# Agent attention and a PReLU layer on one core: sums of exponentials on GpSimd in place of products with ones

## The chip, the cores and the metric

The kernel runs on one core of a Trainium2 chip. The metric is the device time of one execution, in microseconds. Before the change it is 988.02 us, the median of three runs (987.69, 988.02 and 988.49).

## What is computed

Two batches of 12480 queries, keys and values with 128 channels, and 49 agents per batch. The agents gather the values by a softmax over the keys, and each query takes a softmax over the agents. The attention result goes through a layer with 2048 hidden units and a PReLU.

```python
a2k = sm(agents, k)             # softmax over 12480 keys, scale 1/sqrt(128)
agent_v = a2k @ v               # 49 x 128 per batch
q2a = sm(q, agents)             # softmax over 49 agents, per query
x = (q2a @ agent_v).reshape(24960, 128)
h = x @ w_in
g = np.maximum(h, 0.0) + alpha * np.minimum(h, 0.0)
out = g @ w_out
```

In the reference `sm` subtracts the maximum, takes the exponential, and divides by the sum plus 1e-9.

## The kernel before, in words

Because the attention result is linear in the exponentials, the kernel multiplies `agent_v` with `w_in` once per batch (tile `sab`, a rounded part and a remainder), and applies that to the exponentials of the queries. The division by the softmax sum is left to the end: the PReLU is positively homogeneous, so each output row is scaled by the reciprocal of its sum just before it is stored. All products use numbers split in a rounded part and a remainder (`qmh` and `qml` for the exponentials, `rh` and `rl` for the positive part of the hidden units, `wh` and `wl` for the weights).

**Groups, pairs and steps.** The 24960 queries are cut in 52 groups of 480 (`GT`). Two groups make a pair (26 pairs). A group is worked off in eight steps (`NM`), each with 256 of the hidden units, so that there are 416 steps, 16 in a pair. In step s the loop (L1214) emits, in this order: the tasks of `first` for s, `g1(s + 2)`, the tasks of `plan` for s, and `g2(s)`. `g1` (L958) multiplies exponentials with `sab` into a PSUM tile `h` with two buffers (L968), ScalarE takes the positive part `rh` (L974), and VectorE takes the remainder `rl` from `h` and `rh` (L975), which is the last reader of that buffer. `g2` (L980) multiplies `rh` and `rl` with the output weights and adds them up in `acc` over the eight steps (L990); after the last one it adds the linear part (L1001) and brings the sum of both halves to SBUF (L1006 on ScalarE, L1007 on VectorE, tile `os`).

**The chain of a pair.** What prepares the exponentials of pair k is a list of fifteen tasks, `q_chain`, with a list of steps relative to the first step of the pair, `CHAIN` (`CHAIN_0` and `CHAIN_1` for the first two pairs): transpose of the queries (L827), split (L838, L845: `ql`), logits on TensorE (L864), copy to SBUF (L872), a swap of the two halves of the partitions by DMA (L883) and its addition (L890), the maximum over the partitions on GpSimd (L894, `partition_all_reduce`), its subtraction (L899), two exponentials on ScalarE (L903, L908), the split (L912, tile `qml`), the sum (L923), its spread (L933 to L941), and the reciprocal (L946 to L951). `q_take`, `q_swap` and `q_spread` go to `first`, the others to `plan`. Both halves of the partitions hold the same logits after the swap and the addition.

**The sum.** `q_sum` multiplies the two parts of the exponentials with a matrix of ones on TensorE, in two halves of 64 partitions, so that each row of the result holds the sums; `q_spread` copies them from PSUM to the tile `qsum` on ScalarE, and one DMA on SP's queue brings them in a 128x32 tile, from which `q_rec` makes the reciprocals.

**The output.** For group g, `o_take` transposes `os` into `ot` (L1012), `o_scale` multiplies it with the reciprocals (L1017, both operands in SBUF), and `o_store` writes four pieces on SP's queue (L1035). `OUT` says how many steps after the group's end: 4 for `o_take`, 5 for `o_scale` of either group, and one more for `o_store`. Within the 16 steps of a pair, the scaling of its first group falls on step 13 and that of its second group on step 5 of the next pair.

**Beside it.** The first batch's keys and values are worked off ahead of the steps. Those of the second batch are spread over the steps from 16 on: keys in five blocks of 16 steps (transposes L538, products L552, L574, maxima L591), values in six (L618, L609, L632, products L650, L660). Every engine works off its queue in the order in which the tasks are emitted; the tile framework puts in the waits.

Of the kernel before, what the change touches and what calls it, by code (L numbers as in the profile page):

```python
# [9 lines left out]
F32 = mybir.dt.float32  # L10
F32R = mybir.dt.float32r
U32 = mybir.dt.uint32
AF = mybir.ActivationFunctionType
ALU = mybir.AluOpType
# [8 lines left out]
KEYS = (((1, 0), 6, 7), ((5, 3), 9, 14), ((9, 12), 14, 16))  # L23
VALUES = ((((0, 3, 1, 1), (3, 1, 4, 4)), 6), (((3, 0, 7, 8), (2, 8, 5, 6)), 10))
FOLD = (189, 195, 198, 202, 205, 206)
CHAIN = (-18, -16, -16, -14, -13, -13, -11, -10, -7, -6, -5, -5, 4, 5, 10)
CHAIN_0 = (-19, -18, -18, -11, -9, -6, 1, 6, 10, 15, 17, 19)
CHAIN_1 = (-14, -13, -13, -11, -10, -10, -10, -10, -8, -7, -5, -5, 4, 5, 10)
EARLY = (1, 3, 6, 6)
OUT = (4, 5, 5)  # L30


LAGS = (7, 12, 17, 20, 21, 24)
# [22 lines left out]
def kernel(  # L56
# [11 lines left out]
    nc = tc.nc  # L68
# [4 lines left out]
    P = 128  # L73
    HALF = 64
    NF = DFF // P
    GT = 480
    TB = GT // 32
# [13 lines left out]
    SCALE = 1.0 / math.sqrt(C)  # L91
# [5 lines left out]
    p1 = ctx.enter_context(tc.tile_pool(name="p1", bufs=1))  # L97
# [12 lines left out]
    def pair_tile(name, i=None):  # L110

        i = (step[0] // NM + 1) % 2 if i is None else i
        return late[i].tile([P, 2, 512], F32, tag="x", name=name)
# [21 lines left out]
    padb = const.tile([P, 1], F32, name="padb")  # L135
# [654 lines left out]
    NGT = B * NG  # L790
    gq = {}
# [20 lines left out]
    def flat(t):  # L812
        return t.rearrange("p h n -> p (h n)")
# [90 lines left out]
        gq["mh", k] = m  # L904

    def q_exp(k):
        e = gq["e", k] = gq.pop(("s", k))
        nc.scalar.activation(out=e, in_=e, func=AF.Exp, bias=padb, scale=SCALE)  # L908

    def q_split(k):  # L910
        m = p2.tile([P, 2, GT], F32R, tag="qml", name=f"qml{k}")
        nc.vector.tensor_tensor(out=m, in0=gq["e", k], in1=gq["mh", k], op=ALU.subtract)  # L912
        mh = gq.pop(("mh", k))
        gq.pop(("e", k))
        gq["mhl", k] = (m, mh)
        for i in range(2):
            gq["M", 2 * k + i] = (mh[:, i, :], m[:, i, :])

    def q_sum(k):
        t = gq["sum_ps", k] = pair_tile(f"qsum{k}")  # L920
        for n, x in enumerate(gq.pop(("mhl", k))):
            for i, (r0, r1) in enumerate(TILES):
                nc.tensor.matmul(  # L923
                    t[:, i, 0:GT], lhsT=ones[r0:r1, :], rhs=x[r0:r1, i, :],
                    start=n == 0, stop=n == 1,
                )

    def q_spread(k):
        if "sums" not in gq:
            t = gq["sums"] = p1m.tile([P, 1024], F32, tag="qsum", name="qsum")  # L930
            nc.gpsimd.memset(t[:, 2 * GT :], 1.0)
        t = gq["sums"]
        nc.scalar.copy(  # L933
            out=t[:, 0 : 2 * GT].rearrange("p (h n) -> p h n", h=2),
            in_=gq.pop(("sum_ps", k))[:, :, 0:GT],
        )

        x = p1m.tile([P, 32], F32, tag="qx", name=f"qx{k}")
        nc.sync.dma_start(
            out=x, in_=t.rearrange("(c o) (i j) -> c o i j", c=4, j=32)[:, 0, :, :]  # L940
        )  # L941
        gq["sum", k] = x

    def q_rec(k):
        t = p1m.tile([P, 32], F32, tag="qst", name=f"qst{k}")
        nc.vector.transpose(out=t, in_=gq.pop(("sum", k)))  # L946
        r = p2.tile([P, 2, TB, 1], F32, tag="qr", name=f"qr{k}")
        nc.vector.tensor_scalar(
            out=r.rearrange("p h t o -> p (h t o)"), in0=t[:, 0 : 2 * TB], scalar1=1e-9, scalar2=None, op0=ALU.add
        )  # L950
        nc.vector.reciprocal(out=r, in_=r)  # L951
        for i in range(2):
            gq["r", 2 * k + i] = r[:, i]
# [68 lines left out]
    def o_store(g):  # L1022
# [14 lines left out]
    q_chain = [  # L1037
        q_transpose, q_hi, q_lo, q_logits, q_take, q_swap, q_add, q_max,
        q_sub, q_exp_hi, q_exp, q_split, q_sum, q_spread, q_rec,
    ]  # L1040

# [5 lines left out]
    with tc.manual_schedule():  # L1047
# [10 lines left out]
        def at(s, f, *a):  # L1058
            plan.setdefault(s, []).append((f, a))
# [34 lines left out]
        for n in range(7):  # L1094
            load, ops = (load_win, narrow_win) if n < 4 else (load_wo, narrow_wo)
            s = SLABS[n]
# [11 lines left out]
        def more():  # L1108
            f = next(loads, None)
            if f is not None:  # L1110
                f[1](*f[2:])
            return f

        while n_in < N_IN:
            f = more()
            n_in += f[1] not in (q_load_rows, load_alpha, load_late)
        for s in range(max(plan) + 1):
            for f, a in plan.pop(s, ()):
                f(*a)
                if f.__name__ == "total" or f in (k_turn, k_mix):  # L1120
                    while True:
                        f = more()
# [5 lines left out]
        p1m = ctx.enter_context(tc.tile_pool(name="p1m", bufs=1))  # L1128
# [22 lines left out]
        for i2 in range(NGT // 2):  # L1151
            s0 = 2 * NM * i2
            if i2 == 0:
                at(10, q_sum, 0)
                pre(11, q_spread, 0)
                at(13, q_rec, 0)
                continue
            steps = CHAIN if i2 > 1 else CHAIN_1
            if i2 > 1:
                at(max(0, s0 - LEADS[2]), q_load, i2)  # L1160
            for f, i in zip(q_chain, steps):
                (pre if f in (q_take, q_swap, q_spread) else at)(s0 + i, f, i2)
        for g in range(NGT):
            s0 = g * NM
            at((g + 1) * NM + OUT[0], o_take, g)
            d = OUT[1 if g % 2 == 0 or g == NGT - 1 else 2]
            at((g + 1) * NM + d, o_scale, g)
            at((g + 1) * NM + d + 1, o_store, g)

# [86 lines left out]
```

## Time and profile before

| | |
|---|---|
| median of three runs | 988.02 us |
| lowest and highest run | 987.69 and 988.49 us |
| span of the profiled execution, first to last instruction | 985.9 us |
| TensorE, VectorE, ScalarE, GpSimd busy | 99%, 85%, 64%, 9% |
| mean granted TensorE clock | 0.998 |

The span is that of one profiled execution; the page lists no other time for it, and a run's time holds the launch and the end around such a span. Busy shares are averages over stages: a plain pair of groups, a pair with keys of the second batch beside it, and a pair with values beside it differ. Matmuls are pipelined and two of 64 rows run at once, so their listed durations overlap. Spans on GpSimd are rough.

### The profile page before, as it was taken

Reading aid. Unit: us, or ns where it says so; the run is one execution under the profiler, and the core shown is the slowest. Engines: PE = TensorE matmul, PEld = TensorE weight load, DVE = VectorE, ACT = ScalarE, POOL = GpSimd, SP = SyncE. Lnnn points to the kernel's source line nnn. Section 1 sums busy time; section 2 is a strip of 40 time slices with the busy share of each in tenths; the row PEclk is TensorE's granted clock in tenths of the full one; section 3 lists DMA queues with packets and bytes.
Section 4 is the critical chain, followed back from the end, with each engine's and each line's share of the span. In section 5 each row is a group of like instructions: output and inputs, shape, how many; then the busy total and the mean of one; then the engine's idle time right before and its main releaser. Section 6 shows DMA issues by size and latency. Waiting matters only on the chain.

```text
span 985.9 us, 21716 instructions
## 1 busy us (share of the span) xinstructions
PE 971.7 (99%) x9046; PEld 927.0 (94%) x9046; DVE 837.7 (85%) x1054; ACT 626.4 (64%) x779; POOL 89.8 (9%) x67
## 2 busy tenths in 40 slices
PE   8989999999999999999999999999999999999997
PEld 5658999999989999999987999999999999999997
DVE  7887988998899999999987788788878887888775
ACT  5765655655667767777765666666666666666563
POOL 0011011011011011001101101100110111011100
PEclk9999999999999999999999999999999999999999
DMA  9933354444234234234312222212221223121201
GB/s 342 361 51 63 65 84 87 81 70 88 42 75 80 62 73 95 45 70 95 65 31 44 42 51 41 53 37 46 52 53 31 42 55 56 35 41 33 42 11 31
DMA packets 281027, 69.51 MB, mean 71 GB/s; under 512 B 259119, under 2 KB 273953, under 8 KB 280929
## 3 DMA queue, kind: packets, MB, share of 16 engines
q1 hardware_dynamic: 279937, 68.00, 33.0%
q8 instruction: 71, 1.16, 0.5%
q10 hardware_dynamic: 992, 0.12, 0.1%
q14 instruction: 27, 0.22, 0.1%
HBM read 42.59 MB, written 12.78 MB: 56 GB/s over the span
## 4 chain that ended last, share of the span: by engine, by line
PE 94%; DVE 2%; DMA 2%; ACT 1%; issue 0%; SPq 0%; ACTq 0%
PE acc L990 55%; PE h L968 27%; PE lg L864 2%; PE kl L552 2%; PE acc L1001 2%; PE av L650 1%; PE qsum L923 1%; DMA kw<-in_k_dram 1%; DMA win<-in_moe_w_in_dram 1%; PE a_ps L726 0%; DVE red L414 0%; PE avw L471 0%; PE ktp L388 0%; PE lin_ps L784 0%; PE etp L451 0%
## 5 line engine op out<-in xcount | busy, mean ns | idle before, releaser
L975 DVE SCALAR_TENSOR_TENSOR rl<-h,rh 128x960 fp32r<-128x960 f32 x416 | 478.2, 1150 | 123.1 <-ACT rh L974 120.8
L974 ACT ACTIVATE rh<-h 128x960 fp32r<-128x960 f32 x416 | 404.3, 972 | 270.1 <-PE h L968 262.1
L968 PE MATMUL h<-qmh,sab 64*128 64x480 f32 x1664 | 401.3, 378 | 0.7 <-DVE rl L975 0.5
L990 PE MATMUL acc<-rh,wl 64*128 64x480 f32 x1664 | 400.3, 378 | 0.0
L990 PE MATMUL acc<-rh,wh 64*128 64x480 f32 x1664 | 398.0, 375 | 0.0
L990 PE MATMUL acc<-rl,wh 64*128 64x480 f32 x1664 | 313.2, 377 | 0.0
L968 PEld LDWEIGHTS h<-qmh,sab 64*128 64x128 f32 x1664 | 247.2, 185 | 7.5 <-DVE rl L975 2.5
L990 PEld LDWEIGHTS acc<-rh,wl 64*128 64x128 f32 x1664 | 246.9, 184 | 5.9 <-issue 2.3
L990 PEld LDWEIGHTS acc<-rh,wh 64*128 64x128 f32 x1664 | 247.6, 184 | 2.9
L990 PEld LDWEIGHTS acc<-rl,wh 64*128 64x128 f32 x1664 | 223.6, 184 | 3.2
L968 PE MATMUL h<-qml,sab 64*128 64x480 f32 x832 | 222.7, 377 | 0.0
L894 POOL PARTITION_ALL_REDUCE qm<-qs x26 | 85.6, 3293 | 768.0 <-DVE qs L890 731.3
L968 PEld LDWEIGHTS h<-qml,sab 64*128 64x128 f32 x832 | 128.0, 185 | 1.7 <-DVE qml L912 0.2
L1006 ACT COPY os<-acc 128x480 f32<-128x480 f32 x52 | 29.2, 561 | 33.8 <-PE acc L1001 33.6
L1007 DVE TENSOR_TENSOR os<-acc,os 128x480 f32<-128x480 f32 x52 | 33.9, 651 | 2.7 <-ACT os L1006 2.4
L1012 DVE STREAM_TRANSPOSE ot<-os 128x480 f32<-128x480 f32 x52 | 34.7, 668 | 0.0
L903 ACT ACTIVATE qmh<-qs,padb 128x960 fp32r<-128x960 f32 x26 | 28.5, 1097 | 9.2 <-DVE qs L899 9.2
L1017 DVE TENSOR_TENSOR ot<-ot,qr 128x480 f32<-128x480 f32 x52 | 33.6, 645 | 0.1
L899 DVE TENSOR_TENSOR qs<-qs,qm 128x960 f32<-128x960 f32 x26 | 29.8, 1148 | 0.5 <-POOL qm L894 0.5
L890 DVE TENSOR_TENSOR qs<-qs,qw 128x960 f32<-128x960 f32 x25 | 28.7, 1148 | 1.7 <-DMA qw<-qs 1.7
L912 DVE TENSOR_TENSOR qml<-qs,qmh 128x960 fp32r<-128x960 f32 x26 | 29.8, 1148 | 0.0
L827 DVE STREAM_TRANSPOSE qt<-qin 128x960 f32<-128x960 f32 x25 | 29.2, 1167 | 0.0
(172 smaller groups left out, 802.8 us busy)
## 6 DMA issues: line engine op xcount, KB each, us to landing
out_dram<-ot SPq DMA_DIRECT2D x206, 60.0 KB
qin<-in_q_dram SPq DMA_DIRECT2D x200, 60.0 KB
qw<-qs SPq DMA_DIRECT2D x50, 240.0 KB
kw<-in_k_dram SPq DMA_DIRECT2D x12, 512.0 KB
vw<-in_v_dram SPq DMA_DIRECT2D x12, 512.0 KB
kb<-in_k_dram SPq DMA_DIRECT2D x96, 64.0 KB
v<-in_v_dram SPq DMA_DIRECT2D x24, 256.0 KB
win<-in_moe_w_in_dram SPq DMA_DIRECT2D x4, 512.0 KB
```

The lines of the kernel that those rows point to most:

```text
L827: nc.vector.transpose(out=flat(t), in_=gq.pop(("in", k)).rearrange("p h t i -> p (h t i)"))
L894: nc.gpsimd.partition_all_reduce(flat(t), flat(gq["s", k]), P, ReduceOp.max)
L899: nc.vector.tensor_tensor(out=t, in0=t, in1=gq.pop(("m", k)), op=ALU.subtract)
L912: nc.vector.tensor_tensor(out=m, in0=gq["e", k], in1=gq["mh", k], op=ALU.subtract)
L968: nc.tensor.matmul(h[:, u, 0:GT], lhsT=w[a][r0:r1, f0 : f0 + P], rhs=x[r0:r1, :], start=n == 0, stop=n == 2,)
L974: nc.scalar.activation(out=rh, in_=h[:, :, 0:GT], func=AF.Relu)
L975: nc.vector.scalar_tensor_tensor(out=rl, in0=h[:, :, 0:GT], scalar=0.0, in1=rh, op0=ALU.max, op1=ALU.subtract)
L990: nc.tensor.matmul(acc[:, i, 0:GT], lhsT=a[r0:r1, 2 * m + u, :], rhs=x[r0:r1, u, :], start=m == 0 and n == 0, stop=False,)
L1006: nc.scalar.copy(out=t, in_=acc[:, 0, 0:GT])
L1007: nc.vector.tensor_tensor(out=t, in0=acc[:, 1, 0:GT], in1=t, op=ALU.add)
L1012: nc.vector.transpose(out=t.rearrange("p t i -> p (t i)"), in_=oo.pop(g))
L1017: nc.vector.tensor_tensor(out=t, in0=t, in1=gq.pop(("r", g)).to_broadcast([P, TB, 32]), op=ALU.mult)
```

## The change

`q_exp` writes the exponentials to a tile of their own for every pair but the first. `q_sum` of these pairs no longer multiplies with ones: a GpSimd copy of one column of `qml` makes GpSimd wait for the split, and a `partition_all_reduce` with addition over all 128 partitions follows and writes `qsum`. Since both halves hold the same numbers the result is twice the sum, and `q_rec` multiplies it by one half. `q_spread` keeps its DMA and loses its copy. `q_sum` moves from step 4 of the pair to step -5 (the step of the split, behind it), and `q_spread` from step 5 to step 1. The scaling of a pair's first group moves from five to nine steps after the group's end (from step 13 of the pair to step 1 of the next one), and its stores with it, except in the last pair.

```diff
-CHAIN = (-18, -16, -16, -14, -13, -13, -11, -10, -7, -6, -5, -5, 4, 5, 10)
+CHAIN = (-18, -16, -16, -14, -13, -13, -11, -10, -7, -6, -5, -5, -5, 1, 10)
-CHAIN_1 = (-14, -13, -13, -11, -10, -10, -10, -10, -8, -7, -5, -5, 4, 5, 10)
+CHAIN_1 = (-14, -13, -13, -11, -10, -10, -10, -10, -8, -7, -5, -5, -5, 1, 10)
-OUT = (4, 5, 5)
+OUT = (4, 9, 5)
...
     def q_exp(k):
-        e = gq["e", k] = gq.pop(("s", k))
-        nc.scalar.activation(out=e, in_=e, func=AF.Exp, bias=padb, scale=SCALE)
+        s = e = gq.pop(("s", k))
+        if k:
+            e = p1.tile([P, 2, GT], F32, tag="qm", name=f"qe{k}")
+        gq["e", k] = e
+        nc.scalar.activation(out=e, in_=s, func=AF.Exp, bias=padb, scale=SCALE)
...
+    def sums():
+        if "sums" not in gq:
+            t = gq["sums"] = p1m.tile([P, 1024], F32, tag="qsum", name="qsum")
+            nc.gpsimd.memset(t[:, 2 * GT :], 1.0)
+        return gq["sums"]
+
     def q_sum(k):
+        e = gq.pop(("e", k))
+        if k:
+            m, _ = gq.pop(("mhl", k))
+            gate = p1m.tile([P, 1], F32, tag="gate", name=f"gate{k}")
+            nc.gpsimd.tensor_copy(gate, m[:, 1, GT - 1 : GT])
+            nc.gpsimd.partition_all_reduce(sums()[:, 0 : 2 * GT], flat(e), P, ReduceOp.add)
+            return
         t = gq["sum_ps", k] = pair_tile(f"qsum{k}")
...
     def q_spread(k):
...
-        nc.scalar.copy(
-            out=t[:, 0 : 2 * GT].rearrange("p (h n) -> p h n", h=2),
-            in_=gq.pop(("sum_ps", k))[:, :, 0:GT],
-        )
+        t = sums()
+        if k == 0:
+            nc.scalar.copy(
+                out=t[:, 0 : 2 * GT].rearrange("p (h n) -> p h n", h=2),
+                in_=gq.pop(("sum_ps", k))[:, :, 0:GT],
+            )
...
         nc.vector.tensor_scalar(
-            out=r.rearrange("p h t o -> p (h t o)"), in0=t[:, 0 : 2 * TB], scalar1=1e-9, scalar2=None, op0=ALU.add
+            out=r.rearrange("p h t o -> p (h t o)"), in0=t[:, 0 : 2 * TB], scalar1=0.5 if k else 1.0, scalar2=1e-9,
+            op0=ALU.mult, op1=ALU.add,
         )
...
-            d = OUT[1 if g % 2 == 0 or g == NGT - 1 else 2]
+            d = OUT[1 if g % 2 == 0 and g < NGT - 2 else 2]
```

## Rows read from the trace of the kernel before

**Rows 1.** The page: busy us (share of the span) xinstructions of each engine.

```profile
PE 971.7 (99%) x9046; PEld 927.0 (94%) x9046; DVE 837.7 (85%) x1054; ACT 626.4 (64%) x779; POOL 89.8 (9%) x67
```

**Rows 2.** The chain that ended last, by line, share of the span.

```profile
by line: PE acc L990 55.4%; PE h L968 27.5%; PE lg L864 2.2%; PE kl L552 2.1%; PE acc L1001 1.9%; PE av L650 1.2%; PE qsum L923 1.2%; DMA kw<-in_k_dram 1.1%; DMA win<-in_moe_w_in_dram 0.7%; PE a_ps L726 0.5%; DVE red L414 0.5%; PE avw L471 
```

**Rows 3.** Busy time of each engine in three stretches: plain, keys, values.

```profile
core 0: us, PE busy (x) PEld busy (x) DVE busy (x) ACT busy (x) POOL busy (x), PEclk, DMA share, GB/s
596.70:630.00 33.30, 33.30 (x310) 33.27 (x308) 27.47 (x31) 21.13 (x23) 3.31 (x1) 1.00 0.26 47
161.10:199.80 38.70, 38.70 (x408) 38.62 (x407) 34.69 (x43) 22.63 (x26) 3.33 (x2) 1.00 0.48 81
311.60:346.70 35.10, 35.10 (x341) 35.04 (x338) 33.25 (x45) 25.69 (x35) 3.50 (x5) 1.00 0.36 74
```

**Rows 4.** Instructions of tile qsum: min/median/max ns, first and last start us, form.

```profile
L923 PE MATMUL qsum<-qml,ones x52: 372/378/383, 95.0 to 956.3; 64*128 64x480 f32 x52
L923 PE MATMUL qsum<-qmh,ones x52: 371/377/383, 95.2 to 956.5; 64*128 64x480 f32 x52
L933 ACT COPY qsum<-qsum x26: 942/954/958, 97.4 to 957.4; 128x960 f32<-128x960 f32 x26
```

**Rows 5.** Timeline of PE, plain pair: start us, us, engine, line, operation.

```profile
820.96 0.38 PE L968 MATMUL h<-qmh,sab 64*128 64x480 f32 x1
...
822.92 0.38 PE L968 MATMUL h<-qmh,sab 64*128 64x480 f32 x1
...
825.32 0.38 PE L968 MATMUL h<-qmh,sab 64*128 64x480 f32 x1
```

**Rows 6.** Line L894's reduces on GpSimd, and two rows of GpSimd's timeline.

```profile
L894 POOL PARTITION_ALL_REDUCE qm<-qs x26: 3043/3314/3318, 51.4 to 929.8; - x26
...
346.75 3.31 POOL L894 PARTITION_ALL_REDUCE qm<-qs  x1 [27.21 <-DVE qs L890]
...
49.22 0.23 POOL L239 CAST aq<-aq 64x64 fp32r<-64x64 f32 x1 [47.30 <-DVE aq L235]
```

**Rows 7.** Timeline of DVE, values pair, around the maximum on GpSimd.

```profile
347.08 1.15 DVE L975 SCALAR_TENSOR_TENSOR rl<-h,rh 128x960 fp32r<-128x960 f32 x1
348.14 0.88 DVE L632 TENSOR_TENSOR e<-s,e 128x196 fp32r<-128x196 f32 x1
...
352.31 0.35 DVE L632 TENSOR_TENSOR e<-s,e 128x196 fp32r<-128x196 f32 x1
```

**Rows 8.** Timeline of DVE, plain pair, from the split on.

```profile
807.58 1.15 DVE L912 TENSOR_TENSOR qml<-qs,qmh 128x960 fp32r<-128x960 f32 x1
...
811.35 0.64 DVE L1017 TENSOR_TENSOR ot<-ot,qr 128x480 f32<-128x480 f32 x1
...
817.47 1.15 DVE L845 TENSOR_TENSOR ql<-qt,qh 128x960 fp32r<-128x960 f32 x1
818.54 1.15 DVE L975 SCALAR_TENSOR_TENSOR rl<-h,rh 128x960 fp32r<-128x960 f32 x1
820.33 1.16 DVE L975 SCALAR_TENSOR_TENSOR rl<-h,rh 128x960 fp32r<-128x960 f32 x1 [0.64 <-ACT rh L974]
```

**Rows 9.** Timeline of DVE, start of a keys pair.

```profile
189.84 1.13 DVE L975 SCALAR_TENSOR_TENSOR rl<-h,rh 128x960 fp32r<-128x960 f32 x1
190.88 0.70 DVE L538 STREAM_TRANSPOSE kt<-kb 128x512 f32<-128x512 f32 x1
191.49 1.12 DVE L975 SCALAR_TENSOR_TENSOR rl<-h,rh 128x960 fp32r<-128x960 f32 x1
```

**Rows 10.** Timeline of PE, the same keys pair.

```profile
193.10 0.43 PE L968 MATMUL h<-qmh,sab 64*128 64x480 f32 x2
```

**Rows 11.** Timeline of DVE, start of a values pair.

```profile
373.19 1.15 DVE L975 SCALAR_TENSOR_TENSOR rl<-h,rh 128x960 fp32r<-128x960 f32 x1
```

**Rows 12.** Timeline of PE, the same values pair.

```profile
374.94 0.49 PE L968 MATMUL h<-qmh,sab 64*128 64x480 f32 x2
```

**Rows 13.** Timeline of SP's queue, plain pair: swap, then stores.

```profile
787.89 1.12 SPq L883 DMA_DIRECT2D qw<-qs  x2
...
812.02 1.94 SPq L1035 DMA_DIRECT2D out_dram<-ot  x4
```

**Rows 14.** Timeline of DVE: the addition that reads what the swap brought.

```profile
795.27 1.15 DVE L890 TENSOR_TENSOR qs<-qs,qw 128x960 f32<-128x960 f32 x1
```

More of the change, by code (lines that the diff above doesn't have):

```diff
@@ L913, in q_split @@
         mh = gq.pop(("mh", k))
-        gq.pop(("e", k))
         gq["mhl", k] = (m, mh)
@@ L928, in q_spread @@
     def q_spread(k):
[L929 to L932, printed above, removed]
-        nc.scalar.copy(
-            out=t[:, 0 : 2 * GT].rearrange("p (h n) -> p h n", h=2),
-            in_=gq.pop(("sum_ps", k))[:, :, 0:GT],
-        )
+        t = sums()
[4 more added lines that the diff above has]
+            )
         x = p1m.tile([P, 32], F32, tag="qx", name=f"qx{k}")
```

## The prediction

> **What bounds the kernel now.** I read the busy times first. TensorE is busy 971.7 of 985.9 us [rows 1]: it is the wall, and VectorE with 85% is the next. The chain that ended last says the same, and gives the products with ones 1.2% of the span [rows 2]. Then I read the busy times by stage, one stretch per pair of groups: a plain pair late in the kernel, a pair with keys of the second batch, a pair with its values [rows 3]. TensorE is full in all three, but VectorE is not equally close behind: 27.47 of 33.30, 34.69 of 38.70 and 33.25 of 35.10 us. With values under way 1.85 us per pair are left on VectorE, so there a freed TensorE is worth what VectorE can follow. Last I read the timelines for single steps, for where in a pair that slack lies.
>
> The loop to keep in mind: a step writes its products into one of two PSUM buffers, ScalarE takes the positive part, VectorE the remainder (rl), and only then may TensorE write that buffer again, two steps later. TensorE waits as soon as an rl ends after the step that wants its buffer is due.
>
> **The products removed.** 25 of 26 pairs lose four matmuls each (the first pair keeps them). A matmul is listed with 378 ns [rows 4], but two run at once and follow each other closely, so I price by steps: a plain step goes from 820.96 to 822.92, 1.96 us; the one that holds the products, from 822.92 to 825.32, takes 2.40 [rows 5]. That is 0.44 us each, all of it on the wall (the chain's 1.2% over 26 would give 0.455). 25 x 0.44 = **11.0 us off**. ScalarE loses 25 copies of 954 ns [rows 4]; at 64% it is not the wall, so I count 0 for them.
>
> **The sum on GpSimd.** Added per pair: one copy of one column, and an all-reduce with add over 128x960. No row shows that add. The nearest is the maximum of the same shape, 3.31 us (3.04 at least) [rows 6]. From below I take 3.04 us. From above: a GpSimd cast of 64 columns takes 0.23 us [rows 6], so 960 columns take some 3.5 us a pass, and an add that passed them once for each of the seven doublings of 128 rows would need about 24 us; that is an estimate. I take 3.3 us, the nearest row by far. GpSimd is busy 9% [rows 1], so the length itself costs nothing: the split ends at 808.73 (807.58 + 1.15), the transfer of the sums is due six steps (some 12 us) later, and the reciprocal nine steps after that. The copy waits for the split; queued behind it on GpSimd are only this sum, the next pair's maximum eleven steps later, and the small fills for the values, which come five steps later at the earliest.
>
> A page speaks against handing this to GpSimd. The row comes first: 128x960 in 3.31 us. The Trainium skill, "GPSIMD Engine Reference", section 3.2, gives 247.7 us for a reduction over partitions of 128x2048; for 960 columns an estimate from it is 116 us. By that GpSimd would be the wall at some 3 ms (25 times 119 us, the sum and the maximum); the trace disagrees for the maximum, and no run here yet shows the add.
>
> **What the sum does to VectorE.** During the maximum from 346.75 to 350.06 [rows 6], an rl (one operand in PSUM) kept its 1.15 us, while a subtraction with both operands in SBUF took 0.88 instead of 0.35 us [rows 7]: 0.53 us lost per such operation. In the 3.3 us after the split only rl, the transpose of the output and, 2.6 us after its end at 811.35, the scaling of the first group [rows 8] are in the queue; the last has two SBUF operands, and the change moves it away. So nothing in the window is of the slowed kind: 0. If it hit one all the same, 0.53 us per pair, which a plain pair covers and a values pair does not.
>
> The Trainium skill, "SBUF — State Buffer", section "SBUF: two separate sides", says that such an instruction and a GpSimd instruction that reads SBUF exclude each other for a whole instruction. The trace agrees on which kind is slowed and not on the length: the slowed one ended at 349.02, 1.04 us before the listed end of the maximum. By the rule a caught operation would lose up to 3.3 us instead of 0.53.
>
> **The scaling, moved four steps.** 25 scalings of 0.64 us [rows 8] leave the stretch after the split, and come between two rl at the start of the next pair, behind ql. In a plain pair VectorE idles 0.64 us just there, before the rl at 820.33 [rows 8]: 0, and if the cover were gone, 0.64 us against a slack of half a microsecond. In a keys pair there is no idle: the rl that would be pushed starts at 191.49 and ends at 192.61 [rows 9], and TensorE wants its buffer at 193.10 [rows 10]: slack 0.49, so with the hand-over about 0.2 us of wait. Five blocks of keys: 1.0 us. In a values pair the rl ends at 374.34 (373.19 + 1.15) [rows 11], wanted at 374.94 [rows 12]: 0.60, so about 0.1 us; six blocks: 0.6 us. From below, 0, because VectorE is also relieved of 0.64 us thirteen steps into the pair. Together **1.6 us back**, between 0 and 5.
>
> **The queues.** On SP the transfer of the sums comes four steps earlier, and the four stores of the first group four steps later, which puts 1.94 us of issues just ahead of the swap of the next pair [rows 13]. The swap is issued at 787.89 and its reader starts at 795.27 [rows 13, 14]; 7.4 us less 1.9 leave 5.5, so 0. If that did not suffice, the wait would be a fraction of a microsecond per pair. The stores wait for the scaling, and loads of keys queued behind them are issued seven steps ahead of use. The multiplier in the reciprocal is a second scalar in an instruction already there: 0.
>
> **Sum.** -11.0 + 1.6 = -9.4 us. The profiled span goes from 985.9 to 976.5. The page gives no other time for that execution; the three runs, 987.69 to 988.49, stand 1.8 to 2.6 us above its span, and the median 988.02 becomes 978.6.
>
> **The rivals.** *VectorE keeps the gain in the crowded stages.* For it: 33.25 of 35.10 us busy in a values pair; against: its idle time is still over a microsecond after 0.44 us are gone. Five keys pairs and six values pairs then give back all of their 0.44: 4.8 us more than nothing, with the 1.6 us on top 6.4; 988.0 - 11.0 + 6.4 = 983.4.
>
> *The add is slow and holds VectorE.* The next operation with two SBUF operands after the split is ql at 817.47, 8.7 us after the split's end [rows 8]. At up to 8.7 us the sum is hidden. Beyond it ql waits, then every rl behind it; the buffers give half a microsecond, 0.6 at most, and 0.44 are saved. So the sign turns at about 9.7 us, three times the maximum. At 10 us: 1.3 - 0.6 - 0.44 = 0.26 us lost per pair, 25 times 6.5: 994.5. For it: no row of the add, and the slowing of rows 7; against: the same shape and data movement at 3.31 us, and a price per caught operation of 0.53, which the buffers absorb. It needs ql to wait until the sum's end.
>
> The lock told on "SBUF — State Buffer" in the Trainium skill is the rule by which this rival would bite, and the 116 us that I scaled from "GPSIMD Engine Reference" would be its far end; the trace so far bears out neither, the first only in a weaker form.
>
> *The products were hidden anyway*, and something else sets the length of a step, so the time stays at 988. Against it: the step with the products is 0.44 us longer, with TensorE never idle in it.
>
> **How the numbers follow.** Forecast 0.70, gain kept by VectorE 0.14, slow add 0.10, hidden anyway 0.06. A measurement of this kernel tells about 0.2%, some 2 us, from no change. Faster: 0.70 + 0.14 = 0.84; same 0.06; slower 0.10. The forecast's own range is 976.6 (11.4 us at the chain's price, none back) to 982.0 (5 us back); with the first rival it reaches to 984.0, and 0.16 is left outside above it. Below I go to 976.2.
>
> **What would show it.** In the profile after: 100 fewer matmuls, the step with the products 1.96 us long, a plain pair 32.86 instead of 33.30 us; 25 sums of about 3.3 us on GpSimd, starting right behind the splits; rl unchanged at 1.15 us inside them; the moved scaling at 0.64 us ahead of an rl that started after an idle gap; waits of TensorE for rl of a few tenths at the start of the keys and values pairs. The prediction is wrong if sums last over 9 us, if ql or the scaling grows longer, or if the pairs with keys and values do not shorten.

## The result, and the profile after

The changed kernel takes 998.98 us, the median of four runs (998.01 to 1001.88), against 988.22 before (four runs, the three of the first section and one more): 1.0118 times, interval 1.0106 to 1.013. It is slower, by 10.8 us; 978.6 was forecast, and the range ended at 984.0.

The page of the changed kernel: span, busy times of part 1, and the row of part 2 with the granted clock of TensorE in 40 slices.

```profile
span 1000.1 us, 21538 instructions
PE 979.3 (98%) x8946; PEld 907.2 (91%) x8946; DVE 839.9 (84%) x1054; ACT 606.8 (61%) x754; POOL 237.5 (24%) x117
PEclk9999989989899999999999999999999999999999
```

The hundred matmuls are gone ([rows 1] has 9046), and GpSimd works 2.6 times as long. New are three slices with an 8 in the clock's row, all in the first third: something made TensorE stand there. The waits of the changed kernel say what (who waited for whom: us in total, times, longest):

```profile
DVE kt L538 <- DMA kb<-in_k_dram: 13.2, 4, 3.6
PEld h L982 <- DVE rl L989: 13.6, 14, 2.8
PE h L982 <- DVE rl L989: 8.4, 5, 2.4
DVE qs L890 <- DMA qw<-qs: 6.4, 6, 1.3
```

The first of these did not exist before: the transpose of a block of keys waits for its load, with up to 3.6 us, and it stands in VectorE's queue ahead of an rl, for which TensorE then waits. To see where in the kernel the time went I measured each pair from one maximum on GpSimd (L894) to the next, in the traces of all kernels of this study but e6. The profiled execution of the changed kernel is its longest run (1001.88 us), so the table shows some 3 us more of loss than the median:

| us | before | changed | e1 | e2 | e3 | e4 | e5 | e7 | e8 | e9 |
|---|---|---|---|---|---|---|---|---|---|---|
| five keys pairs, sum | 185.8 | 206.6 | 186.3 | 185.2 | 201.9 | 192.5 | 185.9 | 185.2 | 186.4 | 185.2 |
| six values pairs, sum | 210.4 | 209.1 | 212.0 | 208.7 | 211.0 | 209.1 | 217.1 | 208.4 | 211.0 | 208.7 |
| one plain pair | 33.31 | 33.01 | 33.77 | 33.01 | 33.31 | 33.01 | 34.23 | 33.01 | 33.31 | 33.01 |

All of the loss lies in the five pairs with keys, 20.9 us; every plain pair gained 0.30 us, and the six pairs with values gained 1.3 us together (one of them lost 0.43).

One of the five, in the changed kernel. VectorE's timeline first, then SP's queue, then TensorE's matmuls into `h`:

```profile
158.76 0.64 DVE L1031 TENSOR_TENSOR ot<-ot,qr 128x480 f32<-128x480 f32 x1
...
165.21 0.71 DVE L538 STREAM_TRANSPOSE kt<-kb 128x512 f32<-128x512 f32 x1 [3.08 <-DMA kb<-in_k_dram]
165.85 1.12 DVE L989 SCALAR_TENSOR_TENSOR rl<-h,rh 128x960 fp32r<-128x960 f32 x1
...
169.93 1.16 DVE L890 TENSOR_TENSOR qs<-qs,qw 128x960 f32<-128x960 f32 x1 [1.34 <-DMA qw<-qs]
```

```profile
159.43 1.95 SPq L1049 DMA_DIRECT2D out_dram<-ot  x4
161.42 4.23 SPq L528 DMA_DIRECT2D kb<-in_k_dram  x8
165.75 1.16 SPq L883 DMA_DIRECT2D qw<-qs  x2
```

```profile
167.02 0.49 PE L982 MATMUL h<-qmh,sab 64*128 64x480 f32 x2 [1.72 <-DVE rl L989]
```

Read them in this order. The scaling ends at 159.40. SP has waited for it with the four stores, and issues them from 159.43 to 161.38. Only then come the loads of keys, two blocks of four pieces each, at 161.42. The first block is transposed from 165.21 on, 3.08 us late, the rl behind it ends at 166.97, and TensorE goes on at 167.02. The swap, behind the loads, leaves at 165.75, and its reader at 169.93 is late as well, by 1.34 us.

### The profile page after: what moved, and what is told of

Read it like the earlier page. It is cut to its first block, busy times and chain, and to the rows that moved or that the text cites. A ratio compares the mean times of both kernels' runs of the same rounds, so it can differ in the third digit from the quotient of the medians.

```text
span 1000.1 us, 21538 instructions
## 1 busy us (share of the span) xinstructions
PE 979.3 (98%) x8946; PEld 907.2 (91%) x8946; DVE 839.9 (84%) x1054; ACT 606.8 (61%) x754; POOL 237.5 (24%) x117
## 3 DMA queue, kind: packets, MB, share of 16 engines
q8 instruction: 70, 1.15, 0.5%
## 4 chain that ended last, share of the span: by engine, by line
PE 86%; DVE 6%; DMA 3%; SPq 2%; ACT 2%; issue 1%; POOL 0%; DVEq 0%; ACTq 0%; POOLq 0%
PE acc L1004 50%; PE h L982 25%; PE kl L552 2%; DVE rl L989 2%; PE lg L864 2%; PE acc L1015 2%; PE av L650 1%; DMA vw<-in_v_dram 1%; ACT rh L988 1%; DMA kb<-in_k_dram 1%; DMA kw<-in_k_dram 1%; SPq L528 1%; DVE kt L538 1%; SPq L1049 1%; PE a_ps L726 0%
## 5 line engine op out<-in xcount | busy, mean ns | idle before, releaser
L982 PE MATMUL h<-qmh,sab 64*128 64x480 f32 x1664 | 392.2, 381 | 8.7 <-DVE rl L989 8.4
L1004 PE MATMUL acc<-rh,wh 64*128 64x480 f32 x1664 | 392.0, 381 | 0.0
L1004 PE MATMUL acc<-rl,wh 64*128 64x480 f32 x1664 | 306.3, 380 | 0.0
L982 PEld LDWEIGHTS h<-qmh,sab 64*128 64x128 f32 x1664 | 238.6, 186 | 23.3 <-DVE rl L989 13.6
L1004 PEld LDWEIGHTS acc<-rh,wl 64*128 64x128 f32 x1664 | 238.5, 186 | 11.2 <-issue 2.7
L1004 PEld LDWEIGHTS acc<-rh,wh 64*128 64x128 f32 x1664 | 239.5, 186 | 7.5
L1004 PEld LDWEIGHTS acc<-rl,wh 64*128 64x128 f32 x1664 | 212.8, 186 | 8.8
L982 PE MATMUL h<-qml,sab 64*128 64x480 f32 x832 | 214.5, 380 | 0.0
L894 POOL PARTITION_ALL_REDUCE qm<-qs x26 | 85.9, 3305 | 421.0 <-DVE qs L890 384.4
L933 POOL PARTITION_ALL_REDUCE qsum<-qe x25 | 143.7, 5748 | 0.2 <-issue 0.2
L982 PEld LDWEIGHTS h<-qml,sab 64*128 64x128 f32 x832 | 121.5, 186 | 3.9 <-DVE qml L915 0.2
```

Of the source, the lines that this page charges most:

```text
L894: nc.gpsimd.partition_all_reduce(flat(t), flat(gq["s", k]), P, ReduceOp.max)
L933: nc.gpsimd.partition_all_reduce(sums()[:, 0 : 2 * GT], flat(e), P, ReduceOp.add)
L982: nc.tensor.matmul(h[:, u, 0:GT], lhsT=w[a][r0:r1, f0 : f0 + P], rhs=x[r0:r1, :], start=n == 0, stop=n == 2,)
L1004: nc.tensor.matmul(acc[:, i, 0:GT], lhsT=a[r0:r1, 2 * m + u, :], rhs=x[r0:r1, u, :], start=m == 0 and n == 0, stop=False,)
```

## The experiments

The theory after the result, A: the four stores of a pair's first group, now at step 2, hold up what stands behind them in SP's queue in the keys pairs. Rival B: the sum on GpSimd holds VectorE. Rival C: the scaling itself, put between two rl, does.

**e1_scale_back.** The sums stay on GpSimd; scaling and stores go back to where they were.

```diff
-OUT = (4, 9, 5)
+OUT = (4, 5, 5)
```

> The changed kernel with the scaling and the stores of every group five and six steps after its end, as before; the sums stay on GpSimd. Theory A (SP's queue: the four stores of the first group, moved to step 2 of a pair, stand ahead of a load of keys whose transpose is due one step later): the stalls of the five keys pairs go, which are 4.7, 6.5, 3.3, 4.8 and 1.5 us, 20.9 in all; what is left is the 0.3 us saved in each other pair, some 7 us, less what the scaling loses as it now meets the 5.75 us sum (0 to 0.5 us per pair where VectorE is full): 978 to 983 us. Rival B (the sum itself, of 5.75 us, holds VectorE): the scaling is now caught as well, so 999 us or more.

Measured: 995.92 us, ratio to before 1.0079 (1.0064 to 1.0094). Neither figure came. The keys pairs are whole again (186.3 us), as A has it, but a plain pair now takes 33.77 instead of 33.01 us. VectorE and GpSimd of e1, in a plain pair:

```profile
816.04 1.12 DVE L989 SCALAR_TENSOR_TENSOR rl<-h,rh 128x960 fp32r<-128x960 f32 x1
817.08 2.35 DVE L1031 TENSOR_TENSOR ot<-ot,qr 128x480 f32<-128x480 f32 x1
819.36 1.15 DVE L989 SCALAR_TENSOR_TENSOR rl<-h,rh 128x960 fp32r<-128x960 f32 x1
```

```profile
814.68 5.75 POOL L933 PARTITION_ALL_REDUCE qsum<-qe  x1
```

The scaling, caught by the sum, takes 2.35 instead of 0.64 us, while the rl before it, inside the same sum, keeps 1.12. So 1.7 us are lost, where I had priced 0.53, and the buffers absorb only a part: a plain pair is 0.76 us longer than in the changed kernel. Both halves of the change belong together: with the scaling at its old place the sum costs more than it saves.

**e2_stores_later.** Only the stores move, behind the loads and the swap.

```diff
-            at((g + 1) * NM + d + 1, o_store, g)
+            at((g + 1) * NM + d + (3 if d == OUT[1] else 1), o_store, g)
```

> The changed kernel with only the stores of the first group of a pair two steps later (step 4 of the pair in place of 2), behind the loads of keys of step 2; the scaling stays at step 1, the sums on GpSimd. Theory A: 976 to 982 us, no wait of a transpose of keys for its load. Rival C (it is the scaling itself, put between two rl at the start of a pair, that stalls VectorE and TensorE in the keys pairs): 996 to 1000 us. Rival B: 996 to 1000 us.

Measured: 980.47 us, ratio 0.9925 (0.991 to 0.994), faster than both kernels. No wait of a transpose for its load is left among its waits, and the keys pairs take 185.2 us. The 18.5 us between it and the changed kernel are the place of four DMAs per pair. B and C, which expected 996 or more, fall as causes of this loss.

**e3_move_alone and e8_scale_alone.** The kernel before with the move alone: in e3 scaling and stores, in e8 the scaling with the stores behind the loads. Both have the products on TensorE. From e3 to e8:

```diff
 OUT = (4, 9, 5)
...
-            at((g + 1) * NM + d + 1, o_store, g)
+            at((g + 1) * NM + d + (3 if d == OUT[1] else 1), o_store, g)
```

> The kernel before with only the scaling and the stores of the first group moved four steps, as in the change; the products with ones stay on TensorE. Theory A: the 20.9 us of the keys pairs come, and nothing is saved: 1005 to 1010 us. Rival B (the sum on GpSimd holds VectorE): 987 to 990 us. Rival C: also 1005 to 1010, so this run tells only B from the other two.

> The kernel before with the scaling of the first group at step 1 of the next pair, and its stores at step 4, behind the loads and the swap (e3_move_alone with only the stores two steps later); products with ones on TensorE. Theory A: 986 to 990 us, so that the 17 us of e3 belong to the stores in SP's queue. Rival C: 1000 us or more, since the scaling sits where it sat in e3.

Measured: e3 1005.32 us (1.0175, 1.016 to 1.019), e8 988.99 us (1.0011, 1.0002 to 1.0021). Both are as A expected; B falls with e3, and C with e8. Without any sum on GpSimd the stores cost 16 us, and the scaling at its new place about one: the keys pairs of e8 are 0.6 us longer in all than before, and the values pairs 0.5.

**e4_loads_first.** All of the change, but where loads and stores of a first group fall on the same step, the loads are issued first.

```diff
+        held = {s: [x for x in t if x[0] is o_store and x[1][0] % 2 == 0] for s, t in plan.items()}
+        for s, t in plan.items():
+            t[:] = [x for x in t if x not in held[s]]
...
+        for s, t in held.items():
+            plan[s] = plan.get(s, []) + t
         for s in range(NS):
```

> The changed kernel with nothing moved but the order inside a step: where a load of keys or values and the stores of a first group fall on the same step, the load is issued first. The scaling stays at step 1, the stores at step 2. Theory A: 976 to 983 us, the keys pairs at or below their 38.65 us. Rivals B and C: 996 to 1000 us.

Measured: 988.06 us, ratio 1.0003 (0.9993 to 1.0012): only 11 of the 18.5 us come back, so that neither A's figure came nor that of B and C. No transpose waits for its load any more: the loads were the larger part of it. The rest stands in VectorE's and SP's timelines of e4:

```profile
163.37 1.16 DVE L890 TENSOR_TENSOR qs<-qs,qw 128x960 f32<-128x960 f32 x1 [2.37 <-DMA qw<-qs]
```

```profile
152.59 4.13 SPq L528 DMA_DIRECT2D kb<-in_k_dram  x8
156.76 2.10 SPq L1049 DMA_DIRECT2D out_dram<-ot  x4
158.96 1.18 SPq L883 DMA_DIRECT2D qw<-qs  x2
```

The swap now stands behind eight loads and four stores, 2.1 us later than without the stores, and its reader waits 2.37 us; over the kernel 13.0 us in six waits, where the trace of before has 1.7 us in two. In a plain pair there are no loads of keys ahead of it, and it is early enough.

**e5_two_sums.** On top of e2 the sum is taken twice in a row, to tell how long it holds VectorE.

```diff
             nc.gpsimd.partition_all_reduce(sums()[:, 0 : 2 * GT], flat(e), P, ReduceOp.add)
+            nc.gpsimd.partition_all_reduce(sums()[:, 0 : 2 * GT], flat(e), P, ReduceOp.add)
```

> e2_stores_later with the sum on GpSimd taken twice in a row (the second writes the same numbers over the first), 25 more all-reduces of 5.75 us, so that GpSimd holds on for some 11.5 us after the split, past the start of ql 8.7 us after the split. Theory X (while the sum reads, an instruction of VectorE with two SBUF operands waits until about one us before the listed end of the sum): ql waits 1 to 3 us in every pair, the buffers absorb 0.6, so 0.5 to 2 us per pair over the 980.5 of e2: 992 to 1030 us, and ql is listed with 2 to 4 us. Rival Y (such an instruction only loses about 0.5 us, as the prediction priced it): 980 to 985 us, and ql is listed with at most 1.7 us. GpSimd as the wall is excluded: 11.5 + 3.3 us in a pair of 33.

Measured: 1004.18 us (1.0161, 1.0146 to 1.0176), 23.7 us over e2. ql is caught and takes 2.71 us, as X said, and a plain pair takes 34.23 us. VectorE, then GpSimd:

```profile
831.10 2.71 DVE L845 TENSOR_TENSOR ql<-qt,qh 128x960 fp32r<-128x960 f32 x1
```

```profile
822.57 0.18 POOL L932 COPY gate<-qml 128x1 f32<-128x1 f32 x1 [9.13 <-DVE qml L915]
822.72 5.75 POOL L933 PARTITION_ALL_REDUCE qsum<-qe  x1
828.55 5.75 POOL L934 PARTITION_ALL_REDUCE qsum<-qe  x1
```

In four of the keys pairs ql starts 4.6 us after the second sum's start. It keeps its 1.15 us there, and the keys pairs are hardly longer than in e2 (185.9 against 185.2).

**e6_no_gate.** On top of e2 the copy that makes the sum wait for the split is left out.

```diff
-            gate = p1m.tile([P, 1], F32, tag="gate", name=f"gate{k}")
-            nc.gpsimd.tensor_copy(gate, m[:, 1, GT - 1 : GT])
```

> e2_stores_later without the GpSimd copy that waits for the split, so that the sum may start as soon as the exponentials are there, which is when the split (two SBUF operands) starts too. Theory X: in pairs where the sum starts first, the split waits some 4 us, rl and TensorE behind it: up to 3.5 us per pair, 1000 to 1070 us; where the split is first, nothing. Rival Y: 980 to 986 us.

Measured: 1119.89 us (1.1338, 1.1316 to 1.1359), worse than either theory said, by the mechanism of X. The sum starts 0.03 us ahead of the split, and the split takes 5.23 us instead of 1.15. VectorE, GpSimd, and TensorE's clock by stretches of 2 us (the last columns are clock, DMA share and GB/s):

```profile
800.31 5.23 DVE L915 TENSOR_TENSOR qml<-qe,qmh 128x960 fp32r<-128x960 f32 x1
```

```profile
800.28 5.75 POOL L931 PARTITION_ALL_REDUCE qsum<-qe  x1 [7.66 <-ACT qe L911]
```

```profile
803.00:805.00 2.00, 0.04 (x1) 0.00 (x0) 2.00 (x1) 0.00 (x0) 2.00 (x1) 1.00 0.00 0
805.00:807.00 2.00, 0.34 (x2) 0.34 (x4) 2.00 (x3) 0.00 (x0) 1.03 (x1) 0.72 0.00 0
807.00:809.00 2.00, 2.00 (x12) 1.66 (x12) 1.23 (x2) 0.73 (x1) 0.00 (x0) 0.50 0.05 8
809.00:811.00 2.00, 2.00 (x14) 1.66 (x12) 1.73 (x2) 0.24 (x1) 0.00 (x0) 0.50 0.00 0
811.00:813.00 2.00, 2.00 (x16) 1.68 (x14) 0.64 (x2) 0.97 (x1) 0.00 (x0) 0.58 0.00 0
```

TensorE waits 3.62 us for an rl, until 806.66, and then runs at 0.50 of its clock, its lower level of 1.2 GHz, until some 5 us after the wait. The lower clock comes on top of the wait: a plain pair takes 38.3 to 39.5 us here against 33.01 in e2, at least 5.3 us more, where the split lost 4.1.

**e7_scale_at_7.** The other way out: the changed kernel with the scaling at step 15 of the pair, and its stores at step 0, two steps ahead of the loads.

```diff
-OUT = (4, 9, 5)
+OUT = (4, 7, 5)
```

> The changed kernel with the scaling of the first group seven steps after its end (step 15 of the pair) and its stores at step 0 of the next pair, two steps ahead of the load of keys. Theory A with X: the sum has stopped holding VectorE by step 15 (it is listed for 5.75 us from just after the split, under three steps and a transpose later), and the stores are issued before the loads and the swap: 977 to 982 us. Rival C (a scaling beside ql stalls VectorE): the keys and values pairs get slower by up to a microsecond each, 985 to 992 us.

Measured: 981.38 us, ratio 0.9932 (0.9916 to 0.9949), as A with X expected and not to be told from e2. The scaling takes 0.66 us there at the longest, and the keys pairs take 185.2 us. So it was not the move of the scaling that cost (in e2 it sits as late as in the changed kernel), but the step to which its stores went along.

**e9_no_sum.** Why a plain pair gained 0.30 and not 0.44 us: e2 with no sum at all from the third pair on; the sums of the second pair are used again, so that part of the computation is left out.

```diff
+            if k > 1:
+                return
             gate = p1m.tile([P, 1], F32, tag="gate", name=f"gate{k}")
```

> e2_stores_later with the sums left out from the third pair on (neither products nor GpSimd; the sums of the second pair are used again, so the output is scaled by the wrong numbers). It tells why a plain pair went from 33.31 only to 33.01 us and not to 32.87. Theory P (the products were worth 0.30 us and not the 0.44 by which their own step was longer, because the other steps change when they are gone): a plain pair stays at 33.0, 979 to 982 us. Theory Q (the sum on GpSimd costs 0.14 us per pair): a plain pair takes 32.87, some 977 us.

Measured: 981.12 us (0.993, 0.9914 to 0.9947), the same as e2, as theory P expected. GpSimd's maxima in plain pairs of e9 follow each other by 33.01 us, as in e2, with no sum between them:

```profile
593.89 3.31 POOL L894 PARTITION_ALL_REDUCE qm<-qs  x1 [29.70 <-DVE qs L890]
626.90 3.32 POOL L894 PARTITION_ALL_REDUCE qm<-qs  x1 [29.70 <-DVE qs L890]
```

So the sum behind the gate costs nothing that these runs can tell, and the products with ones were worth 0.30 us per pair.

## Why the prediction was wrong

**The queues: this step failed.** I wrote that "loads of keys queued behind them are issued seven steps ahead of use". Seven is the lead that the code asks for; but a load also waits until the block three before it has been transposed, since `kb` has three buffers. For one block in six that leaves one step: the block that is turned at step 3 of a pair takes the buffer of the one turned at step 1, and is loaded at step 2. That is the very step to which the stores moved. The swap was checked in a plain pair alone, and with too much cover. The 7.4 us run from its issue to its reader, and I took off only the stores, not the swap's own time, which is 4.2 us where the reader waits for it (issue at 165.75, reader at 169.93 in the changed kernel). So a plain pair had some 3 us to spare and about 1.2 behind the stores, not 5.5; that was enough there. A keys pair had next to nothing, since loads stand ahead of the swap. The kernel before, SP and then VectorE:

```profile
155.44 1.17 SPq L883 DMA_DIRECT2D qw<-qs  x2
```

```profile
159.83 1.15 DVE L890 TENSOR_TENSOR qs<-qs,qw 128x960 f32<-128x960 f32 x1
```

These are 4.39 us. Of the 18.5 us by which the place of the stores decides, e4 gives 11 to the loads and leaves 7.6, with the late swaps. e3 shows the same without GpSimd.

My first idea after the result was this one alone, and e1 showed that it wasn't enough: simply undoing the move is no cure.

**The products: right in kind, too large.** 11.0 us were forecast; 0.30 us in each of 25 pairs are 7.5, and e2 has 7.4 (980.47 against 987.9, the median of before beside it; its interval leaves some 6 to 9, so that the about 1 us of the moved scaling is not to be told in it). I took the length of the step that holds the products less a plain one, 0.44 [rows 5]. That step did shrink to the plain length, but the plain steps grew. TensorE, starts of two steps, first of the kernel before and then of the changed one:

```profile
804.19 0.50 PE L968 MATMUL h<-qmh,sab 64*128 64x480 f32 x2
...
806.14 0.50 PE L968 MATMUL h<-qmh,sab 64*128 64x480 f32 x2
```

```profile
819.85 0.45 PE L982 MATMUL h<-qmh,sab 64*128 64x480 f32 x2
...
821.82 0.46 PE L982 MATMUL h<-qmh,sab 64*128 64x480 f32 x2
```

1.97 us, where the steps at the same place of a pair took 1.94 to 1.95 before; over the 16 steps of a pair the growth takes back 0.14 of the 0.44. e9 shows that GpSimd has no part in it. Why the matmuls follow each other a little less closely once the products are gone wasn't tried and stays open.

**The sum on GpSimd: length wrong, place right.** It takes 5.75 us and not the 3.31 of the maximum; the bounds of 3.04 and 24 held it. GpSimd went to 24% with no harm. The rival of the slow add is real, but not at this length: e5, whose sums last until 11.6 us after they start, loses 23.7 us by that mechanism, and e2, with 5.75, nothing.

**What it does to an instruction with two SBUF operands: mis-sized threefold and more.** I priced 0.53 us per caught operation, from one that the maximum had caught late [rows 7]. e1 shows 1.7 us, e6 4.1. In the changed kernel itself neither the split, ql nor the scaling is caught (none is over 1.16 us), so this term did not make the miss. In the three caught cases shown the instruction ran at its usual length once 4.1 us of the sum were over: in e1 the scaling ended at 819.43, so it began at 818.79 at 0.64 us, 4.11 after the sum's start at 814.68; in e6 the split began at 804.39 (805.54 less 1.15), 4.11 after 800.28; in e5 ql at 832.66 (833.81 less 1.15), 4.11 after 828.55. The same holds, within 0.02 us, for all 68 caught instructions of the three traces, which started from 0.02 to 3.6 us into a sum. So it is a full wait and not a slower pace, and it ends 1.64 us ahead of the sum's listed end.

The Trainium skill, "SBUF — State Buffer", section "SBUF: two separate sides", has this rule: such an instruction and one of GpSimd that reads SBUF exclude each other. I had held the trace against it because the caught operation ended before the maximum did; the runs here agree with the rule, but the exclusion ends 1.64 us before the sum's listed end; whether the listed end is late or the last part reads nothing, no run shows. The rule speaks for the gate and for the move. The estimate of 116 us that I scaled from the Trainium skill, "GPSIMD Engine Reference", section 3.2, does not hold for this sum, which takes 5.75 us; the page's figure is for another instruction, `tensor_reduce`.

**The scaling at its new place: right in size.** 1.0 us in the keys pairs and 0.6 in the values pairs were forecast; e8 has 0.6 and 0.5, from one profiled execution of either kernel, and a plain pair unchanged at 33.31.

**The rivals.** VectorE did not keep the gain in the values pairs: they shortened by 0.29 us each in e2. The products were not hidden. The side was missed because the only rival that ended slower was about GpSimd, and the cause sat in a queue that I had put at 0.

## What to carry to other kernels

When a DMA moves in a queue, look up the shortest lead of everything behind it, in every stage, and take that from the buffers and not from the lead that the code asks for: one load in six was due one step later, and four stores ahead of it, which also waited for their data, cost 16 us (e3 against e8) to 18.5 (the change against e2). The sum on GpSimd was free here only where no instruction of VectorE with two SBUF operands started in its first 4.1 us; the copy that makes it wait was worth 139 us (e6 against e2), and the distance of the scaling 15 (e1 against e2). What a removed piece is worth is the difference of whole periods (0.30 us here), and not of the step that held it (0.44).

## What was not expected of the hardware

A wait of TensorE can cost more than its length. In the changed kernel, after a wait of 2.41 us for an rl at 121.93, TensorE's stretches show (busy times of PE, PEld, DVE, ACT, POOL, then the granted clock):

```profile
119.00:121.00 2.00, 0.52 (x6) 0.11 (x2) 0.88 (x2) 0.22 (x1) 0.00 (x0) 1.00 0.79 127
121.00:123.00 2.00, 1.07 (x6) 0.93 (x8) 2.00 (x3) 0.00 (x0) 0.00 (x0) 0.69 0.85 163
123.00:125.00 2.00, 2.00 (x22) 1.93 (x18) 0.72 (x2) 0.97 (x1) 0.00 (x0) 0.50 0.35 121
125.00:127.00 2.00, 2.00 (x20) 2.00 (x20) 2.00 (x3) 0.17 (x1) 0.91 (x1) 0.50 0.03 8
127.00:129.00 2.00, 2.00 (x12) 1.64 (x12) 1.64 (x3) 0.32 (x1) 2.00 (x1) 0.50 0.40 60
129.00:131.00 2.00, 2.00 (x12) 1.64 (x12) 0.00 (x0) 0.45 (x1) 0.41 (x1) 0.50 0.58 91
131.00:133.00 2.00, 2.00 (x16) 1.68 (x16) 1.44 (x2) 0.53 (x1) 0.00 (x0) 0.75 0.74 118
```

At 0.50 it is at 1.2 GHz, its lower level, for some nine microseconds after the wait. So late transfers cost more than they were late: from the maximum at 90.2 to that at 171.2, which holds the first two late loads (3.64 and 3.08 us) and their late swaps (1.28 and 1.34), the changed kernel takes 81.0 us (35.88 and 45.16), and the one before 69.8 (31.17 and 38.64): 11.2 us more, where the four add up to 9.3. The slices with an 8 on the page lie behind the late loads of 120.12, 207.53 and 251.20.

The fifth keys pair, from 257.2 to 296.8, shows that the clock has a part in it. It holds no late load and no wait of TensorE, and still takes 39.60 us, where it took 38.06 before. It begins at the lower clock that the pair ahead of it left behind:

```profile
256.00:258.00 2.00, 2.00 (x14) 1.73 (x14) 2.00 (x3) 0.49 (x1) 0.77 (x1) 0.50 0.00 0
258.00:260.00 2.00, 2.00 (x12) 1.67 (x12) 1.78 (x3) 0.00 (x0) 2.00 (x1) 0.50 0.56 85
260.00:262.00 2.00, 2.00 (x14) 1.66 (x14) 0.98 (x1) 0.97 (x1) 0.55 (x1) 0.57 0.68 106
```

The addition over 128 partitions on GpSimd takes 5.75 us for 960 columns where the maximum takes 3.31, in all 25 pairs within 12 ns (min, median and max in ns, first and last start us):

```profile
L933 POOL PARTITION_ALL_REDUCE qsum<-qe x25: 5744/5748/5756, 100.6 to 956.6; - x25
```
